# Routed experts in longer blocks: a first block of 256 rows, then blocks of up to 512 with the last in six lengths

## The chip, the cores and the metric

The kernel runs on one core of a Trainium2 chip. The metric is device time in microseconds (us) from one launch, the median of several runs. Before the change it is 1612.41 us, over three runs from 1605.84 to 1612.46.

## What is computed

Attention with a feature map, and then two mixtures of experts, one on the output of the other. There are 4608 tokens (8 batches of 576) of 512 values; each mixture has 8 experts with 512 x 1024 and 1024 x 512 weights, all in 32-bit floats, and a token goes to the one expert with the largest logit.

```python
def phi(x):                                   # attention
    proj = np.einsum('bhsd,df->bhsf', x, w_phi)
    proj = proj - np.max(np.abs(proj), axis=-1, keepdims=True)
    return np.concatenate([np.exp(proj), np.exp(-proj)], axis=-1)
q_p, k_p = (phi(q), phi(k))
kv = np.einsum('bhsf,bhsd->bhfd', k_p, v)
num = np.einsum('bhsf,bhfd->bhsd', q_p, kv)
den = np.einsum('bhsf,bhf->bhs', q_p, k_p.sum(axis=2))[..., None] + 1e-06
...
e_idx = np.argmax(x @ w_gate, axis=1)         # a mixture; it is applied twice
gate_w = probs[np.arange(N), e_idx]
eom = 1.0 / (1.0 + np.exp(-(x @ w_output_gate)))     # the first mixture alone
for e in range(E):
    mask = e_idx == e
    h = np.maximum(x[mask] @ w1[e], 0.0)
    out[mask] = gate_w[mask, None] * eom[mask, e, None] * (h @ w2[e])
```

## The kernel before, in words

**Stages.** Attention runs to about 495 us of the profiled span, the experts of the first mixture to about 1060, those of the second to the end. Attention also routes its own output: `logits` (L512) multiplies turned rows by the gate weights, `route` finds each token's expert, weight and rank, and `scatter` (L184) writes one table entry for each token into a table in HBM, in the place that the expert and the rank give. An expert's table entries say which rows of x to gather.

**A block.** `gather` (L287) fetches rows, 128 to a tile, by an indirect DMA from GpSimd; `turn` (L294) transposes them on TensorE (L301) and splits them into a high and a low part, on ScalarE (L303) and VectorE (L304). `block` (L307) takes 256 rows, or 128 with the high and low parts side by side. The hidden layer has eight chunks f of 128 units, and for each f and each of four chunks kc of x three matmuls (L328 to L330: high by high, low by high, high by low) or two (L333, L334). ScalarE and VectorE split the relu into hh and hl (L345, L346). The output layer makes 24 matmuls of 512 columns for each tile of 128 rows (L353 to L355); ScalarE multiplies the result by the token's weight (L359) and GpSimd scatters it (L360).

**A tail.** In the first mixture a finished block of two tiles is also routed for the second: `tail` (L369) turns its y (L381), multiplies by the gates (L391), adds up the four partial products with a matrix of ones (L399), lets `route` find places, and scatters two table entries. These steps are hooks in the next block: `hook(i)` runs them between its chunks f (0 to 7) and in its output layer (8 and up).

**The order.** Inside a block the program is put down as written. The first block of each expert carries, at hooks, the split of the next expert's weights (`split_steps`, L240: 8 chunks through four raw buffers, 512 KB each, refilled by SyncE), the turning of its own second block and of the next expert's first, and the gathers for the blocks after these, on GpSimd's queue. There are two sets of weights, `rings`, used in turn (w0.. and w1..). The table of all experts is read back once in a mixture, in `end_route` (L205) in the first block of expert 0.

**The chain of tests.** The number of rows of an expert is known only on the chip. After the first block each engine loads the counts into registers (L455), and `rest` (L466) tests them: more than 512 rows (L476) runs a full block and goes on; otherwise `short` (L482) chooses a block of 128, one of 256, or none. There is code for four such lengths (`FITTED`) and then a row of blocks of 256, each behind one test. Every engine that has work inside runs every test itself, and the code lies in the order of nesting.

Of the kernel before, what the change touches and what calls it, by code (L numbers as in the profile page):

```python
# [21 lines left out]
F32 = mybir.dt.float32  # L22
# [14 lines left out]
SLOTS = N // P  # L37
NG = B // 2
GW = P // KC
NT = 9  # L40
FITTED = 4


class Fused:
# [8 lines left out]
    def consts(self):  # L53
# [24 lines left out]
        self.pend = const.tile([P, 2], I32, name="pend")  # L78


    def new_route(self, name, n_scatter, pool, *gates):
# [13 lines left out]
        return {"name": name, "table": table, "rows": rows, "acc": acc,  # L95
# [94 lines left out]
    def early(self, r, psum):  # L190


        nc, sm = self.nc, self.small
        acc = r["acc"][:, 0:1]
        nc.tensor.matmul(psum[:, :1], self.ones_h, acc, start=True, stop=True)
        few = sm.tile([P, 1], F32, tag="few", name="few", bufs=1)
        nc.vector.tensor_scalar(few, psum[:, :1], float(2 * P), None, op0=ALU.is_lt)
        up = sm.tile([P, 1], F32, tag="up", name="up", bufs=1)
        nc.vector.tensor_scalar(up, acc, -1.0, 2.0, op0=ALU.mult, op1=ALU.add)
        nc.vector.scalar_tensor_tensor(acc, up, few, acc, op0=ALU.mult, op1=ALU.add)  # L200
        first = self.const.tile([P, 2, 2], I32, name=f"{r['name']}_first")
        nc.sync.dma_start(first, r["table"].rearrange("(p s) w -> p s w", p=P)[:, :2, :])
        r["first"] = first

    def end_route(self, r, psum):  # L205
# [3 lines left out]
        cnt = self.const.tile([P, E], I32, name=f"{r['name']}_cnt")  # L209
        bf = sm.tile([P, E], F32, tag="bf", name="bf", bufs=1)  # L210
        nc.vector.tensor_copy(bf, self.base_i)
        nc.vector.scalar_tensor_tensor(cnt, bf, -float(P), psum[:, :E], op0=ALU.mult, op1=ALU.add)
        nc.sync.dma_start(self.tab, r["table"].rearrange("(p s) w -> p s w", p=P))
        r["cnt"] = cnt


    def weight_buffers(self, pool, name):
        return [tuple(pool.tile([P, 1024], F32R, name=f"{name}{c}{x}") for x in "hl") for c in range(8)]
# [21 lines left out]
    def split_steps(self, i):  # L240

        nc = self.nc

        def step(c):
            raw = self.raws[c % 4]
            hi, lo = self.rings[i % 2][c]
# [7 lines left out]
    def weights(self, i):  # L254
        r = self.rings[i % 2]
# [5 lines left out]
    def expert_buffers(self, pool):  # L261

        self.ybuf = [pool.tile([P, D], F32, name=f"y{t}") for t in range(2)]
        self.xt = pool.tile([P, KC, 2 * P], F32, name="xt")
        self.ls = pool.tile([P, 2 * P], F32, name="ls")
        self.xg += [[self.shared.tile([P, D], F32, tag=tag, name=f"xg{i}{t}", bufs=2) for t in range(2)]
                    for i, tag in enumerate(("tl4", "phi1"), 1)]
        self.xbuf.append(pool.tile([P, KC, 2, 2 * P], F32R, name="x1"))
        self.hbuf = [self.shared.tile([P, FC, 2 * P], F32R, tag="phi4", name=f"h{x}", bufs=3) for x in "hl"]
        self.rings.append(self.weight_buffers(pool, "w1"))  # L270
# [560 lines left out]
```

## Time and profile before

| | before |
|---|---|
| median of 3 runs | 1612.41 us (1605.84 to 1612.46) |
| the profiled execution | 1597.7 us, span 1596.0 us |
| mean granted TensorE clock | 0.968 |
| PE (TensorE matmul) busy | 1488.2 us, 93% |
| PEld (weight load) busy | 1316.2 us, 82% |
| DVE (VectorE) busy | 737.0 us, 46% |
| ACT (ScalarE) busy | 589.5 us, 37% |
| POOL (GpSimd) busy | 424.6 us, 27% |
| DMA | 163.15 MB, mean 102 GB/s |

The page of the profile describes one execution; the span runs from its first instruction to its last. PE is TensorE's array, PEld its weight loads (beside the matmuls), PEldq and ACTq and so on the sequencers that feed an engine. A row of the trace names a line of the kernel, an engine, an operation and the tiles as out<-in. "Busy" of a matmul is from its start to a modelled end, so that consecutive ones overlap; the distance of two starts is the better price. "issue" as a releaser is time in which the engine waited for nothing that the profile shows. The granted clock is a share of TensorE's full speed.

### The profile page before, as it was taken

Reading aid. Unit: us, or ns where it says so; the run is one execution under the profiler, and the core shown is the slowest. Engines: PE = TensorE matmul, PEld = TensorE weight load, DVE = VectorE, ACT = ScalarE, POOL = GpSimd, SP = SyncE. Lnnn points to the kernel's source line nnn. Section 1 sums busy time; section 2 is a strip of 40 time slices with the busy share of each in tenths; the row PEclk is TensorE's granted clock in tenths of the full one; section 3 lists DMA queues with packets and bytes.
Section 4 is the critical chain, followed back from the end, with each engine's and each line's share of the span. In section 5 each row is a group of like instructions: output and inputs, shape, how many; then the busy total and the mean of one; then the engine's idle time right before and its main releaser. Section 6 shows DMA issues by size and latency. Waiting matters only on the chain.

```text
span 1596.0 us, 27799 instructions
## 1 busy us (share of the span) xinstructions
PE 1488.2 (93%) x10702; PEld 1316.2 (82%) x10702; DVE 737.0 (46%) x1939; ACT 589.5 (37%) x1199; POOL 424.6 (27%) x433
## 2 busy tenths in 40 slices
PE   7999899899999898998998999998989989998997
PEld 6887787787787797987987889887889879888986
DVE  6787576576665342625444536143144234141310
ACT  5554354354443232414333424132234334142311
POOL 3443533433443212312122212213112012110100
PEclk9999999999998999999999999999999989998999
DMA  7775123123013322404134404114144134131200
GB/s 204 240 244 188 46 61 127 47 67 126 24 38 128 117 70 99 162 24 151 62 115 135 147 26 146 43 41 165 41 155 160 42 125 163 42 116 68 86 19 28
DMA packets 99084, 163.15 MB, mean 102 GB/s; under 512 B 25819, under 2 KB 62043, under 8 KB 97760
## 3 DMA queue, kind: packets, MB, share of 16 engines
q1 hardware_dynamic: 83008, 117.98, 22.8%
q0 software_dynamic: 15776, 41.52, 7.7%
q8 instruction: 146, 2.39, 0.6%
q14 instruction: 154, 1.26, 0.3%
HBM read 118.67 MB, written 42.88 MB: 101 GB/s over the span
## 4 chain that ended last, share of the span: by engine, by line
PE 72%; issue 12%; DMA 9%; POOL 2%; ACT 2%; DVE 2%; SPq 0%; POOLq 0%; another core or an unknown queue 0%; ACTq 0%; DVEq 0%
DMA out_dram<-y,tab 7%; PE hp L328 7%; PE hp L330 7%; PE yp L353 7%; PE yp L355 7%; PE hp L329 7%; PE yp L354 7%; PE nm L672 6%; PE kvt L624 4%; PE pj L589 2%; PE hp L333 2%; PE tp L658 2%; PE pj L591 2%; PE pj L590 2%; PE tp L301 2%
## 5 line engine op out<-in xcount | busy, mean ns | idle before, releaser
L346 DVE SCALAR_TENSOR_TENSOR hl<-hp,hh 128x512 fp32r<-128x512 f32 x148 | 102.3, 691 | 336.1 <-ACT hh L345 336.1
L345 ACT ACTIVATE hh<-hp 128x512 fp32r<-128x512 f32 x148 | 88.5, 598 | 271.4 <-PE hp L330 252.2
L359 ACT ACTIVATE y<-yp,tab 128x512 f32<-128x512 f32 x76 | 52.4, 689 | 290.1 <-PE yp L355 225.2
L184 POOL DMA_INDIRECT r_table<-pay,at x78 | 78.6, 1008 | 291.8 <-DVE at L180 221.2
L360 POOL DMA_INDIRECT out_dram<-y,tab x38 | 38.4, 1010 | 411.0 <-ACT y L359 409.5
L672 PE MATMUL nm<-kvs,qt 128*128 128x65 f32 x1024 | 120.5, 273 | 3.3 <-DVE pre L140 1.5
L672 PEld LDWEIGHTS nm<-kvs,qt 128*128 128x128 f32 x1024 | 118.4, 192 | 4.9 <-issue 2.0
L593 DVE TENSOR_REDUCE am<-pj 128x4 f32<-128x512 f32 (+1 forms) x160 | 100.1, 634 | 33.7 <-PE pj L591 32.7
L594 DVE TENSOR_TENSOR d<-pj,am 128x512 f32<-128x512 f32 (+1 forms) x160 | 96.4, 629 | 2.5 <-PE kvt L624 2.4
L289 POOL DMA_INDIRECT xg<-r_rows,tab x82 | 86.2, 1052 | 40.2 <-issue 22.0
L589 PE MATMUL pj<-wh,th 128*128 128x256 f32 x288 | 88.3, 311 | 2.9 <-ACT th L576 1.5
L383 DVE COPY xt<-tp 128x512 f32<-128x512 f32 x21 | 14.5, 692 | 161.4 <-PE tp L381 161.4
L610 POOL TENSOR_TENSOR fs<-phi 128x512 f32<-128x512 f32 x32 | 40.8, 1275 | 180.7 <-ACT phi L603 147.4
L360 POOL DMA_INDIRECT r_rows<-y,tab x38 | 37.8, 994 | 188.7 <-ACT y L359 179.5
L660 ACT ACTIVATE qt<-tp 128x512 f32<-128x512 f32 (+1 forms) x192 | 79.5, 504 | 16.9 <-PE nm L678 8.3
L612 POOL TENSOR_TENSOR fs<-fs,phi 128x512 f32<-128x512 f32 x64 | 81.9, 1280 | 4.7
L590 PE MATMUL pj<-wl,th 128*128 128x256 f32 x288 | 83.0, 292 | 0.0
L591 PE MATMUL pj<-wh,tl 128*128 128x256 f32 x288 | 82.5, 299 | 0.3
L576 ACT CAST th<-tp 128x512 fp32r<-128x512 f32 (+1 forms) x96 | 42.1, 491 | 77.9 <-PE tp L572 77.8
L304 DVE TENSOR_TENSOR x<-tp,x 128x512 fp32r<-128x512 f32 x86 | 55.4, 683 | 26.6 <-ACT x L303 26.6
L328 PE MATMUL hp<-x,w10h 128*128 128x256 f32 x128 | 41.4, 324 | 27.2 <-issue 26.5
L589 PEld LDWEIGHTS pj<-wh,th 128*128 128x128 f32 x288 | 56.5, 196 | 11.0 <-ACT th L576 5.5
(293 smaller groups left out, 4620.5 us busy)
## 6 DMA issues: line engine op xcount, KB each, us to landing
raw<-in_moe_w_dram SPq DMA_DIRECT2D x128, 512.0 KB, 4.4
r_rows<-zero SPq DMA_DIRECT2D x15, 768.0 KB, 7.4
km<-in_k_dram SPq DMA_DIRECT2D x32, 256.0 KB, 3.0
qm<-in_q_dram SPq DMA_DIRECT2D x32, 256.0 KB, 3.6
vm<-in_v_dram SPq DMA_DIRECT2D x32, 256.0 KB, 3.4
r_rows<-x SPq DMA_DIRECT2D x8, 1024.0 KB, 4.8
xg<-r_rows,tab POOLq DMA_INDIRECT x82, 5.8
r_table<-pay,at POOLq DMA_INDIRECT x78, 2.2
```

The lines of the kernel that those rows point to most:

```text
L328: nc.tensor.matmul(o, w1h[kc][:, fs], x[:, kc, 0, :], start=first, stop=False)
L329: nc.tensor.matmul(o, w1h[kc][:, fs], x[:, kc, 1, :], start=False, stop=False)
L330: nc.tensor.matmul(o, w1l[kc][:, fs], x[:, kc, 0, :], start=False, stop=last)
L346: nc.vector.scalar_tensor_tensor(ol, hp, 0.0, oh.bitcast(F32), op0=ALU.max, op1=ALU.subtract)
L353: nc.tensor.matmul(yp, hh[:, f, sl], w2h[f], start=first, stop=False)
L354: nc.tensor.matmul(yp, hh[:, f, sl], w2l[f], start=False, stop=False)
L355: nc.tensor.matmul(yp, hl[:, f, sl], w2h[f], start=False, stop=last)
L589: nc.tensor.matmul(o, hi[:, i + j, :], wh, start=True, stop=False)
L590: nc.tensor.matmul(o, hi[:, i + j, :], wl, start=False, stop=False)
L591: nc.tensor.matmul(o, lo[:, i + j, :], wh, start=False, stop=True)
L593: nc.vector.tensor_reduce(am, pj, axis=AX.X, op=ALU.max, apply_absolute_value=True)
L672: nc.tensor.matmul(nm[:, t, :], qt[:, s, 4 * b + t, :], kv[:, 2 * b + s, :], start=(s == 0), stop=(s == 1))
```

## The change

- **Lengths.** Each expert's first block keeps 256 rows (`FIRST` tiles), with x in x0. What follows is in blocks of 512 rows, x in one buffer of four tiles, and the last one has 128, 256, 320, 384, 448 or 512 rows; a matmul of the hidden layer spans all of them. `end_route` computes for each expert how many half tiles and tiles are begun beyond the first block; the engines load both numbers.
- **The chain.** `choose` nests the tests: none left, at most 2 half tiles, 4, 5, 6, 7, 8, else a full block and a second choice of four lengths, and behind that a loop over blocks of 512.
- **Rows.** An expert's first block issues, ahead of its own matmuls, the gathers of the next four tiles and turns all four at hooks 10 to 19 (17 to 23 for expert 0). The expert's last block gathers and turns the next expert's first two tiles, at its hooks.
- **Weights.** There are three half sets, which change roles by `chunks`. The first block splits the next expert's w1 at hooks 1 to 7, the last block its w2; if there is none, both happen in `leave`, by themselves.
- **Tails** take the number of tiles of the block before them; ahead of a first block always four, with entries of no token in place of missing tiles. Buffers of y are four, aligned at their end, and set to zero at the start, like the unused parts of h, on GpSimd (`start_buffers`).
- **Logits.** The four partial products are turned by transposes and added by a reduce on VectorE, where a matmul by a matrix of ones did both; in attention (L525) and in the tails (L399).
- In PSUM, hp has three banks of one f each, tp three, yp two; before, hp had two tags of two banks, tp two, yp two.

```diff
     def end_route(self, r, psum):
...
+        nc.vector.tensor_scalar(cf, cf, -float(FIRST * P), 0.0, op0=ALU.add, op1=ALU.max)
+        for i, rows in enumerate((64, P)):
+            n = r["begun"][:, i, :]
+            nc.vector.tensor_scalar(n, cf, float(rows - 1), None, op0=ALU.add)
+            nc.vector.tensor_scalar(n, n, 6 + i, None, op0=ALU.logical_shift_right)
         nc.sync.dma_start(self.tab, r["table"].rearrange("(p s) w -> p s w", p=P))
-        r["cnt"] = cnt
+    def chunks(self, i):
+        sets = self.sets
+        return sets[(0, 2, 1)[i % 3]] + sets[(1, 0, 2)[i % 3]]
...
-        for fp in range(FC // 2):
-            hp = ps.tile([P, 2, 2 * P], F32, tag=f"hp{min(c, 1)}", name="hp", bufs=2)
...
+        for f in range(FC):
+            hp = ps.tile([P, 4 * P], F32, tag="hp", name="hp", bufs=3)
+            fs = slice(f * P, (f + 1) * P)
+            for kc in range(KC):
+                first, last = kc == 0, kc == KC - 1
+                if nt > 1:
+                    o = hp[:, :R]
+                    nc.tensor.matmul(o, w1h[kc][:, fs], x[:, kc, 0, :R], start=first, stop=False)
+                    nc.tensor.matmul(o, w1h[kc][:, fs], x[:, kc, 1, :R], start=False, stop=False)
+                    nc.tensor.matmul(o, w1l[kc][:, fs], x[:, kc, 0, :R], start=False, stop=last)
...
+        turns = {1: (9, 11, 13, 15), 2: (9, 11, 13, 15), 3: (10, 14, 18, 22), 4: (12, 17, 22, 27)}
+        splits = {1: (8, 10, 12, 14), 2: (8, 10, 12, 14), 3: (8, 12, 16, 20), 4: (9, 14, 19, 24)}
...
+        def part(g, t, size, before, final, rows=4):
...
+                if not final:
+                    self.gather(r, self.place(e, t + nt, rows))
+                    at(hooks, turns[nt], turn_steps(rows))
+                elif follow(g):
+                    at(hooks, (0, 0), follow(g))
+                    at(hooks, turns[nt], first_steps)
+                if not m:
+                    at(hooks, (0, 0, 1, 2, 4) if nt > 1 else (0, 0, 2, 4, 6), self.tail(r2, before, ps))
+                if final:
+                    at(hooks, splits[nt], self.split_steps(g + 1)[4:])
+                self.block(self.weights(g), self.x, self.place(e, t, nt), size * 64, dst, ps, hooks, not m)
...
+            def choose(sizes):
+                if not sizes:
+                    part(g, t, 8, before, False)
+                    rest(g, t + 4, done + 8, k, tiles, 4)
+                    return
+                with tc.If(k > done + sizes[0]) as more:
+                    choose(sizes[1:])
+                with more.Else():
+                    if sizes[0]:
+                        last(sizes[0])
+                    else:
+                        leave(g)
+            choose([0, 2, 4, 5, 6, 7, 8] if done == 0 else [2, 4, 6, 8])
...
+                if e:
+                    rows()
+                    at(hooks, (0, 0, 1, 2, 4), tail)
+                    at(hooks, (10, 13, 16, 19), turn_steps(4))
+                else:
+                    at(hooks, (0, 0, 1, 2, 3), tail)
...
+                    at(hooks, (4, 4), (lambda: self.end_route(r, col("cn")), rows))
+                    at(hooks, (17, 19, 21, 23), turn_steps(4))
+                at(hooks, (1, 3, 5, 7), self.split_steps(g + 1)[:4])
...
         for i in range(nt):
-            nc.tensor.matmul(lg[:, i, :], ls[:, i * P:(i + 1) * P], self.chunk_sum[:, :width],
-                             start=True, stop=True)
+            nc.tensor.transpose(lp[:, i * P:(i + 1) * P], ls[:, i * P:(i + 1) * P], self.ident)
+        nc.vector.tensor_reduce(
+            lg, lp.rearrange("p (t c e) -> p t e c", t=nt, c=KC)[:, :, :width, :], axis=AX.X, op=ALU.add)
```

How the rows of an engine move shows at two places, both where expert 1 of the first mixture goes from its first block to the next. First TensorE before the change: the last output matmuls (yp) of the first block, the register load, the first test, and the hidden layer (hp) of the second block with weights w1.. of that expert.

```order
5159 L353 MATMUL yp<-w17h,hh 128x512
5160 L354 MATMUL yp<-w17l,hh 128x512
5161 L355 MATMUL yp<-w17h,hl 128x512
5162 L455 TENSOR_LOAD r_cnt
5163 L476 COMPARE_AND_BRANCH
5164 L328 MATMUL hp<-x_6477,w10h 128x256
5165 L329 MATMUL hp<-x_6477,w10h 128x256
5166 L330 MATMUL hp<-x_6477,w10l 128x256
```

One load and one test stand ahead of the version with a full block of 256 columns. The same place after the change:

```order
4054 L376 MATMUL yp<-w03h,h_6488 128x512
4055 L377 MATMUL yp<-w03l,h_6488 128x512
4056 L378 MATMUL yp<-w03h,h_6490 128x512
4057 L546 TENSOR_LOAD r_begun x2
4058 L515 COMPARE_AND_BRANCH x7
4059 L353 MATMUL hp<-x,w20h 128x512
4060 L354 MATMUL hp<-x,w20h 128x512
4061 L355 MATMUL hp<-x,w20l 128x512
```

Two loads and seven tests now lie between them, and behind the tests stands the version for a full block of 512 that is not the last; each shorter version lies further on, where its test jumps to. Next GpSimd, before the change, in the output layer of that first block: table entries (r_table) of a tail, the scatters (r_rows) of the block's two tiles y, and gathers (xg) of rows.

```order
358 L184 DMA r_table<-pay,at 36864x2 x2
359 L360 DMA r_rows<-y_6469,tab 4609x512
360 L289 DMA xg_6473<-r_rows,tab 128x512
361 L289 DMA xg_6474<-r_rows,tab 128x512
362 L289 DMA xg_6119<-r_rows,tab 128x512
363 L289 DMA xg_6120<-r_rows,tab 128x512
364 L360 DMA r_rows<-y_6470,tab 4609x512
365 L455 TENSOR_LOAD r_cnt
366 L476 COMPARE_AND_BRANCH
```

Four gathers, for the next expert's second block and the first block of the one after it, stand between the two scatters, near the test. After the change:

```order
379 L320 DMA xg_6122<-r_rows,tab 128x512
380 L320 DMA xg_6123<-r_rows,tab 128x512
381 L320 DMA xg_6480<-r_rows,tab 128x512
382 L320 DMA xg_6481<-r_rows,tab 128x512
383 L189 DMA r_table<-pay,at 40960x2 x4
384 L383 DMA r_rows<-y_6484,tab 4609x512
385 L383 DMA r_rows<-y_6485,tab 4609x512
386 L546 TENSOR_LOAD r_begun x2
387 L515 COMPARE_AND_BRANCH x7
```

The four gathers, now for this expert's own next rows, come first, ahead of the tail's four table entries; between the scatters and the tests none is left.

## Rows read from the trace of the kernel before

**Rows 1.** The page, part 4: shares of the chain that ended last.
```profile
PE 72%; issue 12%; DMA 9%; POOL 2%; ACT 2%; DVE 2%; SPq 0%; POOLq 0%; another core or an unknown queue 0%; ACTq 0%; DVEq 0%
```

**Rows 2.** Groups of instructions: line, engine, tiles, xcount, busy us, mean ns, idle before.
```profile
L328 PE MATMUL hp<-x,w00h 128*128 128x256 f32 x168 | 51.9, 309 | 12.0 <-issue 11.4 <-DMA raw<-in_moe_w_dram 0.3 <-DVE lgs L714 0.3
...
L328 PE MATMUL hp<-x,w10h 128*128 128x256 f32 x128 | 41.4, 324 | 27.2 <-issue 26.5 <-PE yp L355 0.6
...
L333 PE MATMUL hp<-x,w00h 128*128 128x256 f32 x32 | 12.1, 378 | 1.5 <-ACT y L359 1.2 <-DVE xg L343 0.2
...
L301 PE MATMUL tp<-ident,xg 128*128 128x128 f32 x344 | 45.9, 275 | 6.8 <-DMA xg<-r_rows,tab 5.7 <-DVE x L304 1.1
...
L525 PE MATMUL lg<-chunk_sum,ls 128*128 128x16 f32 x72 | 10.7, 275 | 3.2 <-ACT ls L523 3.2
...
L383 DVE COPY xt<-tp 128x512 f32<-128x512 f32 x21 | 14.5, 692 | 161.4 <-PE tp L381 161.4
```

**Rows 3.** Stretches: us, busy of PE, PEld, DVE, ACT, POOL, PEclk, DMA share, GB/s.
```profile
637.45:651.03 13.58, 13.58 (x119) 12.99 (x117) 8.74 (x32) 6.75 (x13) 1.93 (x2) 1.00 0.23 75
...
1119.78:1131.27 11.49, 11.49 (x97) 11.49 (x96) 2.08 (x3) 2.48 (x4) 3.10 (x3) 1.00 0.20 70
...
1143.19:1151.00 7.81, 7.58 (x65) 7.43 (x65) 2.27 (x6) 2.95 (x7) 1.01 (x1) 1.00 0.12 42
```

**Rows 4.** Timeline of PE: start us, us, engine, line, operation, tiles.
```profile
1119.78 0.28 PE L328 MATMUL hp<-x,w00h 128*128 128x256 f32 x1
...
1131.17 0.28 PE L330 MATMUL hp<-x,w03l 128*128 128x256 f32 x1
...
1132.08 0.47 PE L353 MATMUL yp<-w04h,hh 128*128 128x512 f32 x1
...
1132.39 0.39 PE L354 MATMUL yp<-w04l,hh 128*128 128x512 f32 x1
...
1142.84 0.39 PE L355 MATMUL yp<-w07h,hl 128*128 128x512 f32 x1
```

**Rows 5.** Stretches again: the expert layers as a whole.
```profile
495.00:1589.60 1094.60, 1025.75 (x6659) 928.38 (x6659) 402.87 (x1057) 351.14 (x664) 216.50 (x211) 0.96 0.29 96
```

**Rows 6.** Waits of PE: waiting, releaser, us in total, times, longest.
```profile
PE hp L333 <- issue: 11.5, 3, 5.3
```

**Rows 7.** Sequencer of PE by line: xcount: shortest/median/longest ns, first to last start; waits.
```profile
L476 PEldq COMPARE_BRANCH  x27: 65/3423/6851, 522.6 to 1558.9; - x27
...
L483 PEldq COMPARE_BRANCH  x1: 6532/6532/6532, 604.7 to 604.7; - x1
...
L476 PEldq COMPARE_BRANCH  x1: 3730/3730/3730, 933.3 to 933.3; - x1
```

**Rows 8.** Timeline of PE at two joints between blocks; wait in brackets.
```profile
611.43 0.55 PE L328 MATMUL hp<-x,w10h 128*128 128x256 f32 x1 [7.12 <-issue]
...
937.12 0.39 PE L355 MATMUL yp<-w07h,hl 128*128 128x512 f32 x1
...
937.56 0.35 PE L333 MATMUL hp<-x,w00h 128*128 128x256 f32 x1
```

**Rows 9.** Stretches at those joints.
```profile
604.30:611.40 7.10, 0.00 (x1) 0.01 (x1) 0.48 (x4) 0.69 (x1) 2.05 (x2) 0.73 0.80 279
...
611.40:615.50 4.10, 4.07 (x23) 4.10 (x24) 0.15 (x1) 0.51 (x1) 0.00 (x0) 0.63 0.03 10
...
934.00:938.00 4.00, 3.95 (x20) 3.05 (x19) 0.00 (x0) 0.41 (x1) 0.10 (x1) 1.00 0.22 74
```

**Rows 10.** Timeline of ACT behind a jump; wait in brackets.
```profile
810.49 0.59 ACT L383 COPY xt<-tp 128x512 f32<-128x512 f32 x1 [5.77 <-issue]
...
1146.36 0.37 ACT L342 COPY xg<-hp 128x256 f32<-128x256 f32 x1 [2.36 <-issue]
```

**Rows 11.** The page, part 6: transfers: xcount, KB each, us from issue to landing.
```profile
raw<-in_moe_w_dram SPq DMA_DIRECT2D x128, 512.0 KB, 4.4
...
xg<-r_rows,tab POOLq DMA_INDIRECT x82, 5.8
```

More of the change, by code (lines that the diff above doesn't have):

```diff
@@ L94, in new_route @@
         nc.vector.tensor_copy(acc, self.base_i)
-        return {"name": name, "table": table, "rows": rows, "acc": acc,
+        own = {x: self.const.tile([P, *shape], I32, name=f"{name}_{x}")
+               for x, shape in (("first", (nt, 2)), ("begun", (2, E)))}
+        return {"name": name, "table": table, "rows": rows, "acc": acc, **own,
                 "gates": self.load_gates(f"{name}_gates", *gates), "views": iter(dram_disjoint_views(table, n_scatter))}
@@ L272, in first_rows @@
     def first_rows(self, r):
[L273 to L274 removed]
+        self.xg = [self.shared.tile([P, D], F32, tag="th4", name=f"xg{t}", bufs=2) for t in range(2)]
+        self.gather(r, r["first"])
     def first_turn(self, ps):
[L277 to L285 removed]
@@ L307, in block @@
-    def block(self, r, weights, x, e, c, nt, dst, ps, hooks, keep):
+        tp = ps.tile([P, KC, P], F32, tag="tp", name="tp", bufs=3)
+        for kc in range(KC):
+            nc.tensor.transpose(tp[:, kc, :], self.xg[t][:, kc * P:(kc + 1) * P], self.ident)
+        o = x[:, :, 0, t * P:(t + 1) * P]
+        nc.scalar.copy(o, tp)
+        nc.vector.tensor_tensor(x[:, :, 1, t * P:(t + 1) * P], tp, o.bitcast(F32), op=ALU.subtract)
+    def block(self, weights, x, place, R, dst, ps, hooks, keep):
@@ L421, in at, with turn_steps, follow @@
                 hooks.setdefault(i, []).append(f)
+        def turn_steps(n):
+            return [lambda t=t: self.turn(t, self.x, ps) for t in range(n)]
+        first_steps = [lambda t=t: self.turn(t, self.x0, ps) for t in range(FIRST)]
+        def follow(g):
+            m, e = divmod(g, E)
+            if g + 1 == 2 * E:
+                return None
+            if e + 1 < E:
+                return (lambda: None), (lambda: self.gather(mixes[m][0], self.place(e + 1, 0, FIRST)))
+            return (lambda: self.early(r2, col("early"))), (lambda: self.gather(r2, r2["first"]))
@@ L488, in experts @@
-            rest(1)
+            tail = self.tail(r2, 4, ps) if 0 < g <= E else []
+            rows = lambda: self.gather(r, self.place(e, FIRST, 4))
+            with tc.manual_schedule():
+                if e:
+                    rows()
+                    at(hooks, (0, 0, 1, 2, 4), tail)
+                    at(hooks, (10, 13, 16, 19), turn_steps(4))
+                else:
+                    at(hooks, (0, 0, 1, 2, 3), tail)
+                    if not m:
+                        at(hooks, [0], [lambda: [scatter() for scatter in left(col("rk"))]])
+                    at(hooks, (4, 4), (lambda: self.end_route(r, col("cn")), rows))
+                    at(hooks, (17, 19, 21, 23), turn_steps(4))
+                at(hooks, (1, 3, 5, 7), self.split_steps(g + 1)[:4])
+                self.block(self.weights(g), self.x0, self.place(e, 0, FIRST) if e else r["first"],
+                           FIRST * P, dst, ps, hooks, not m)
```

310 lines of the change are left out of this document (136 added, 174 removed).

## The prediction

> **What bounds the kernel now.** I read the chain of waits first. TensorE holds 72% of it and "issue", time in which nothing recorded is waited for, 12% [rows 1]. The second view counts TensorE's groups in the two MoE layers [rows 2]. Line 328 multiplies x by the chunk w00h or w10h once for each f, so 168 + 128 records, eight to a block, are 37 blocks of 256 rows; x32 at L333 is four blocks of 128 rows on the first weight set (two more ran on the other). That fits the rows that the router gives each expert, counted from the reference's inputs: 754, 436, 681, 421, 364, 417, 537, 998 in the first MoE and 852, 273, 572, 335, 915, 484, 677, 500 in the second. L301's 344 transposes are 86 gathered tiles turned, two of them before 495; L383's x21 counts the routing tails.
>
> The third view prices an undisturbed block [rows 3]: 11.49 us for the hidden layer of 256 rows, 13.58 with a routing tail in it (so a two-tile tail costs 2.09), 7.81 for 128 rows. The timeline prices one instruction [rows 4]. From 1119.78 to 1131.17 there are 95 steps of 0.120 us for 256 columns; from 1132.08 to 1142.84, 47 steps, the first 0.31 and the rest 0.227, for 512 columns. [...] Between 1131.17 and 1132.39 lie the last hidden matmul (0.12), eight transposes and one output matmul (0.23): 0.87 for the eight, 0.11 each, 0.45 a tile.
>
> The fifth view bounds the expert stretch, 495.0 to 1589.6 [rows 5]. Its dense work by these prices: 37 x 11.49 + 6 x 7.81 + 80 output tiles x 24 x 0.227 + 84 turned tiles x 0.45 + 21 tails x 2.09 = 989.5. The stretch lasted 1094.6, so **105 us are lost**. The idle times say where: 11.4 + 26.5 us wait for "issue" at L328 and 11.5 at L333, ahead of a block's first matmul, and 5.7 for gathered rows [rows 2, 6]. The rest is smaller waits and half clock after them.
>
> "issue" here is a branch. TensorE's sequencer records 65 ns for a test that falls through and 3.4 us in the median for one that jumps [rows 7]. A jump of 3.73 us at 933.3 cost almost nothing: the sequencer had reached it 3.8 us ahead of the last queued matmul (937.12), and the next block began at 937.56 [rows 7, 8]. [...] ScalarE has its own copy of every jump and no such lead: idle 2.4 us when quiet, 5.8 under load [rows 10].
>
> **The change, part by part.** *Hidden layer.* Now 16 first blocks of 256 rows; then by expert 512, 256, 448, 256, 128, 256, 320, 512+256 and 512+128, 128, 320, 128, 512+256, 256, 448, 256. On the line of [rows 4] a matmul of 512, 448, 320 columns takes 0.227, 0.200, 0.147, times 96. Sum: 23 x 11.49 + 4 x 21.8 + 2 x 19.2 + 2 x 14.1 + 4 x 7.81 = 449.2 against 472.0: **-22.8**. Of that, 704 fewer matmuls at 0.013 are 9.4 us; the rest is padding no longer multiplied. [...] The 0.120 and 0.227 [rows 4] are measured in this kernel, with its weight loads between them, so I go by them. The output layer keeps its 80 tiles.
>
> *Turned rows.* Every first block turns four tiles whether the expert has them or not: 106 tiles in the stretch for 84, **+9.9** on TensorE (the copies lie beside matmuls).
>
> *Tails.* Nine of four tiles (eight ahead of first blocks) and eight of two, for 21 of two. Logits by transposes save two of four small products in a two-tile tail: 1.87. For four tiles the matrix work alone is 3.3 (16 transposes, 4 products twice as long, 4 transposes, the ranks), twice a two-tile tail 4.18; the routing chain on VectorE and the weight splits share the same six microseconds, so I take 4.18: 52.6 for 43.9, **+8.7** (0 at the low end).
>
> *Attention.* Twelve times, 3 transposes replace 6 narrow products (72 at L525) [rows 2]: 36 x 0.11, **-4.0**; VectorE's reduce for a copy is off the path.
>
> *Losses.* Each expert is entered by two register loads and a chain of n tests, the last of which jumps over the longer versions. Loads and raw weights now start early: gathers at the head of the first block, the last weight chunk at its hook 7, 11 us ahead of the branch, where such transfers land in 4.4 and 5.8 us [rows 11]. So I take the quiet jump. TensorE then waits 2 x 0.42 (the record of 0.31 and a gap) + 3.4 + 0.2 - 3.83 = 0.6 us, and 0.13 for each of 53 further tests (twice the bare record): 16 x 0.6 + 6.9 = 16.7. In each MoE's first expert the last turn waits for a gather at the block's end, so nothing is queued ahead: 2 x 3.8 = 7.6. ScalarE arrives about 4 us behind the last matmul, and a tail's fourth tp bank needs its copy: 2.1 us in the 256-row blocks of the first MoE, 0.4 at 512, 12 in all, and 4 for 128-row blocks of the second. Exits: TensorE's jump hides behind its queue as at 937; far ones leave ScalarE late for four tails, 4 x 1.3 = 5. Three second choices: 4. Gathers: the 5.7 of before and 2 x 1.0 for two more scatters that GpSimd issues ahead of the table (1.93 for two) [rows 3]: 8. Half clock: twelve waits of the kind of 611 at 4.1 x (1 - 0.63) = 1.5 us: 18. Sum 75.3 for 105: **-29.7**. Bounds: 50, if jumps cost what 937 did; 112, if nothing is gained and loads and tests come on top. 75 lies nearest the quiet rows because what loads the DMA engines moves away.
>
> New memsets on GpSimd fall into its pauses while it waits for the last scatters; they cost nothing unless they push the table's load, 2 us at most. A third weight set moves the w2 splits into the last block, beside matmuls; eight copies of 0.59 and two evictions alike [rows 10] fill 5.9 us of ScalarE's time in the 10.9 of a 256-row block's output, and a 128-row one still holds 5.3 in 5.4.
>
> Sum: -22.8 + 9.9 + 8.7 - 4.0 - 29.7 = **-37.9**. The profiled execution took 1597.7, so 1560 by its own measure; the median of the runs, 1612.41, lies 14.7 above it, and I subtract from that: **1574.5 us**.
>
> **Rivals.**
> *Jumps vanish.* All are covered by queued matmuls as at 937: losses 50, 25 less: 1549. For it: the jump at 937 [rows 8]. [...]
> *Nothing gained at the joints.* ScalarE and VectorE, not TensorE's jump, start each block; losses stay at 105 to 112: 1604 to 1611, say 1608. For it: ScalarE's 5.8 us [rows 10].
> *Slower: the jumps stay loaded.* If weights and gathers are still moving when the 16 chains jump (DMA near the 80% of 604.30, not 22%), each takes about 6.1 us in place of 3.4 (43 us), ScalarE is 3.4 later in eight tails (27), and four more entries fall to half clock (6): +76, 1650. For it: 6.53 at 604.7. Against: the transfers' landing times.
> *The fixed cost doesn't shrink.* If the 0.013 us belongs to the columns or the weight load and grows with them, wide matmuls save only a fifth of 9.4 us, 7.5 less: 1582. Against: the two steps, 0.120 and 0.227, where such a cost would give 0.240 [rows 4]. [...]
>
> **How the numbers follow.** Forecast 0.60, vanishing jumps 0.12, nothing gained 0.15, loaded jumps 0.08, fixed cost 0.05. About 0.5%, 8 us, can be told from no change here. Range 1541 to 1610: from vanishing jumps with tails at no extra cost (1549 - 8.7) to the upper end of nothing gained; it leaves out the loaded jumps. Faster by over 0.5% (below 1604.3): the forecast but for 0.01, the vanishing jumps, the fixed cost, and 0.02 of nothing gained: 0.78. Same: 0.13. Slower: 0.09.
>
> **What would show it.** Right: 512-column hidden matmuls 0.227 apart; TensorE's branch records near 3.4 us at the entries with DMA below 30%; "issue" ahead of a block's first matmul about 25 us in all in place of 49; 106 tiles turned. Wrong: entries of 5 us and more; waits of TensorE for ScalarE's xt copies or ranks beyond 20 us; a block of 256 rows with a four-tile tail above 16 us.

## The result and the profile after

The changed kernel takes 1570.67 us in the median of four runs (1567.53 to 1571.97), the kernel before 1609.12 beside it: a ratio of 0.976, 95% interval 0.973 to 0.979. Measured again with 5 runs of its own (the run after_again below) it is 0.981, 0.978 to 0.983. So the change saves some 30 to 39 us; the forecast was 37.9, and 1574.5. The two profiled executions, 1597.7 and 1570.8 us, lie only 27 apart, because the profiled execution of before was 11 us faster than its own median. Terms of the forecast are compared with this pair of traces.

From the page of the changed kernel: the span, the busy shares and the chain that ended last.

```profile
span 1569.0 us, 27135 instructions
...
PE 1468.5 (94%) x10018; PEld 1256.0 (80%) x10018; DVE 766.5 (49%) x2038; ACT 623.7 (40%) x1342; POOL 465.5 (30%) x477
...
PE 60%; DMA 13%; issue 13%; DVE 5%; ACT 4%; POOL 3%; SPq 0%; another core or an unknown queue 0%; POOLq 0%; ACTq 0%; DVEq 0%
```

TensorE issues 684 matmuls less, and the others work a little more. The waits of TensorE answer to [rows 2, 6]:

```profile
PE hp L353 <- ACT y L382: 22.9, 21, 2.2
...
PE hp L353 <- issue: 8.1, 4, 2.2
PE tp L404 <- ACT xt L405: 5.2, 8, 1.8
PE hp L359 <- issue: 4.4, 1, 4.4
...
PE tp L330 <- DMA xg<-r_rows,tab: 4.3, 2, 2.3
```

"issue" ahead of a block's first matmul fell from 49.4 us to 12.5. In its place stand 21 waits put down to ScalarE's eviction of y (L382), which that matmul does not read. They are of two kinds. At thirteen exits (from an expert's last block to the next expert's first) the eviction does end last, 0.05 us ahead of the matmul: a wait that the forecast did not have. At the other eight, all entries (from a first block through the tests behind it), the record of the far jump ends later than the eviction, some 0.2 us ahead of the matmul, so there TensorE waits for the jump, whatever the releaser says. The stretches of single blocks (columns as in [rows 3]), hidden layers of 512, 320, 448 and 512 rows, and the expert layers as a whole, answer to [rows 3, 5]:

```profile
1086.12:1108.40 22.28, 22.06 (x96) 18.04 (x97) 5.51 (x8) 4.18 (x7) 4.85 (x5) 1.00 0.20 60
1217.94:1232.00 14.06, 14.06 (x96) 14.06 (x97) 3.35 (x7) 2.95 (x7) 3.01 (x3) 1.00 0.20 60
1468.11:1487.50 19.39, 19.39 (x96) 17.98 (x97) 4.37 (x7) 3.81 (x7) 2.67 (x3) 1.00 0.15 44
1320.52:1342.20 21.68, 21.68 (x97) 17.98 (x96) 4.84 (x7) 4.87 (x8) 5.11 (x5) 1.00 0.23 61
...
486.00:1559.60 1073.60, 1012.42 (x6011) 875.80 (x6011) 433.02 (x1154) 385.93 (x807) 257.98 (x248) 0.99 0.33 103
```

The wide blocks cost what was forecast (21.8, 14.1, 19.2), and TensorE ran the expert layers at a granted clock of 0.99, where it was 0.96.

The table shows where the 27 us come from, added up over all blocks from the starts of their matmuls (43 blocks before, 35 after). In the second mixture of the kernel before, the first 29 hidden matmuls of the next expert's first block already stand ahead of the test (1181.12 to 1184.47 is one such group, and 4.59 us of "issue" follow it); the wait behind them is counted here as one between blocks, and a normal step between blocks, 0.23 us, is not counted.

| | forecast | traces |
|---|---|---|
| hidden layers, by the prices of single blocks | -22.8 | -22.9 |
| tiles turned | +9.9 | +13.8 |
| attention, to the first hidden matmul (495.03, now 485.97) | -4.0 | -9.1 |
| tails, waits and half clock, in three places: | -21.0 | -11.9 |
| - inside hidden layers (tails among them) | | -1.2 |
| - from a block's last yp matmul to the next block's first hp | | -18.4 |
| - inside output layers (the first block of each mixture: rows not yet there, lower clock) | | +7.7 |
| behind the last matmul (span's end) | 0 | +3.0 |
| rest (rounding) | | +0.1 |
| sum | -37.9 | -27.0 |

### The profile page after: what moved, and what is told of

Read it like the earlier page. It is cut to its first block, busy times and chain, and to the rows that moved or that the text cites. A ratio compares the mean times of both kernels' runs of the same rounds, so it can differ in the third digit from the quotient of the medians.

```text
span 1569.0 us, 27135 instructions
## 1 busy us (share of the span) xinstructions
PE 1468.5 (94%) x10018; PEld 1256.0 (80%) x10018; DVE 766.5 (49%) x2038; ACT 623.7 (40%) x1342; POOL 465.5 (30%) x477
## 3 DMA queue, kind: packets, MB, share of 16 engines
q14 instruction: 191, 1.56, 0.3%
## 4 chain that ended last, share of the span: by engine, by line
PE 60%; DMA 13%; issue 13%; DVE 5%; ACT 4%; POOL 3%; SPq 0%; another core or an unknown queue 0%; POOLq 0%; ACTq 0%; DVEq 0%
DMA xg<-r_rows,tab 6%; PE nm L734 6%; PE yp L376 6%; PE yp L378 6%; PE yp L377 6%; PE hp L353 5%; PE hp L354 5%; PE hp L355 5%; PE kvt L686 4%; DMA out_dram<-y,tab 3%; PE pj L651 2%; PE tp L330 2%; PE pj L653 2%; PE pj L652 2%; PE tp L720 2%
## 5 line engine op out<-in xcount | busy, mean ns | idle before, releaser
L368 DVE SCALAR_TENSOR_TENSOR h<-hp,h 128x256 fp32r<-128x256 f32 (+3 forms) x248 | 116.3, 474 | 376.4 <-ACT h L367 360.0
L367 ACT ACTIVATE h<-hp 128x256 fp32r<-128x256 f32 (+3 forms) x248 | 105.2, 425 | 311.4 <-PE hp L355 249.8
L333 DVE TENSOR_TENSOR x<-tp,x 128x512 fp32r<-128x512 f32 x108 | 74.6, 691 | 168.3 <-ACT x L332 160.4
L189 POOL DMA_INDIRECT r_table<-pay,at x88 | 93.7, 1065 | 209.0 <-DVE at L185 135.2
L320 POOL DMA_INDIRECT xg<-r_rows,tab x104 | 109.6, 1054 | 141.6 <-PE hp L355 49.6
L332 ACT CAST x<-tp 128x512 fp32r<-128x512 f32 x108 | 63.3, 587 | 139.3 <-PE tp L330 120.7
L382 ACT ACTIVATE y<-yp,tab 128x512 f32<-128x512 f32 x76 | 52.3, 688 | 157.8 <-PE yp L378 133.5
L383 POOL DMA_INDIRECT r_rows<-y,tab x38 | 37.9, 997 | 190.4 <-ACT y L382 190.4
L330 PE MATMUL tp<-ident,xg 128*128 128x128 f32 x432 | 65.7, 275 | 4.3 <-DMA xg<-r_rows,tab 4.3
L330 PEld LDWEIGHTS tp<-ident,xg 128*128 128x128 f32 x432 | 54.1, 142 | 19.3 <-issue 3.3
```

The lines of the kernel that those rows point to most:

```text
L320: self.nc.gpsimd.indirect_dma_start(self.xg[t][:, :], None, r["rows"], bass.IndirectOffsetOnAxis(ap=place[:, t, 0:1], axis=0), bounds_chec ...
L330: nc.tensor.transpose(tp[:, kc, :], self.xg[t][:, kc * P:(kc + 1) * P], self.ident)
L367: nc.scalar.activation(oh, o, AF.Relu)
L368: nc.vector.scalar_tensor_tensor(ol, o, 0.0, oh.bitcast(F32), op0=ALU.max, op1=ALU.subtract)
```

## Experiments

Ratios are against the kernel before, on the same chip, with 95% intervals; the changed kernel itself is 0.976 in the first measurement and 0.981 in the second.

**Loads moved back to the tests.** In the main loop, where the first block splits w1:

```diff
-at(hooks, (1, 3, 5, 7), self.split_steps(g + 1)[:4])
+at(hooks, (14, 17, 20, 22), self.split_steps(g + 1)[:4])
```

> The first block splits the next expert's w1 at hooks 14 to 22 in place of 1 to 7, so the refills, four of 512 KB, are on the DMA engines while the tests of the 16 experts are run. Theory: code is fetched by the same engines, so the far jumps at the entries take 5 to 6.5 us in place of 3.3 to 3.9, TensorE waits about 2 us more at each, and some blocks begin at half clock: +30 to +45, 1600 to 1616; the gain of the change over the kernel before is mostly gone. Rival: the jumps of before were slow for another reason (their distance or number), and the entries stay as they are: 1571 within 5.

Measured: 0.9925 (0.9897 to 0.9953), so about two thirds of the gain are gone: 19 to 27 us, short of the 30 to 45 expected. Two entries of the changed kernel, from the start of the far jump to the first matmul behind it, in the view of stretches:

```profile
593.87:597.89 4.02, 2.49 (x11) 1.72 (x10) 0.77 (x3) 1.02 (x2) 0.48 (x1) 1.00 0.02 6
...
1171.76:1175.30 3.54, 2.61 (x12) 1.82 (x11) 0.69 (x1) 1.14 (x2) 0.00 (x0) 1.00 0.02 7
```

The tests there in the records of TensorE's sequencer (columns as in [rows 7]), the far jump the longest:

```profile
L515 PEldq COMPARE_BRANCH  x3: 65/77/3854, 593.6 to 593.9; - x3
...
L515 PEldq COMPARE_BRANCH  x1: 3378/3378/3378, 1171.8 to 1171.8; - x1
```

With the late loads, two entries in the view of stretches:

```profile
733.84:738.96 5.12, 2.08 (x11) 1.38 (x9) 3.13 (x7) 2.69 (x5) 0.98 (x1) 0.93 0.81 256
...
1185.95:1191.31 5.36, 2.26 (x10) 1.53 (x9) 3.10 (x5) 2.87 (x6) 1.01 (x1) 1.00 0.82 259
```

And their jumps in the records of the sequencer:

```profile
L515 PEldq COMPARE_BRANCH  x1: 4950/4950/4950, 733.8 to 733.8; - x1
...
L515 PEldq COMPARE_BRANCH  x1: 5197/5197/5197, 1185.9 to 1185.9; - x1
```

The DMA engines are 2% busy at the entries of the changed kernel and over 80% here, and the same jump takes 5.2 us in place of 3.4 (the second entry of each). Of the thirteen entries with a far jump twelve take 4.2 to 5.2 us; the last expert's, which has no weights to refill, finds the DMA engines 2% busy and takes 3.6. The packets in the trace show where the time goes: each of these four jumps holds one packet of 16 KB on a queue of instructions. At the second entry it begins 1.04 us behind the jump's start in the changed kernel and 2.84 us behind it here, and takes 0.96 us in both. All distances between blocks grow by 20.8 us, and the hidden layers by 10.8, part of it at a lower clock. That is the rival "the jumps stay loaded", brought about by one edit, and it confirms the step that carried the losses: the jumps are cheap because the loads were moved away from them. That a jump waits for this packet is argued from its place inside each of them and from the two delays, 1.04 us at 2% of DMA and 2.84 at 82%; no run shows it by itself.

**Halves.** Each matmul of over 256 columns becomes two:

```diff
+cut = [0, R] if R <= 2 * P else [0, R // 2, R]
+for a, b in zip(cut, cut[1:]):
+    for kc in range(KC):
...
-o = hp[:, :R]
+        o = hp[:, a:b]
```

> Each hidden layer of over 256 rows is computed in two halves of its columns, one after the other, so 8 blocks have 96 matmuls more each, and nothing else changes. If a matmul pays 13 ns beside its columns, as forecast: 768 x 0.013 = +10, 1581. [...] If the price of 256 columns is proportional, 0: 1571.

Measured: 1.0007 (0.9969 to 1.0045), 30 to 40 us above the changed kernel, not 10. Stretches of a hidden layer of 512, 320 and 448 rows, in halves:

```profile
1356.92:1379.90 22.98, 22.98 (x193) 22.97 (x192) 4.84 (x7) 4.87 (x8) 5.12 (x5) 1.00 0.22 58
...
1231.55:1270.30 38.75, 37.49 (x192) 37.45 (x193) 3.44 (x7) 3.06 (x7) 3.06 (x3) 0.57 0.07 23
1509.18:1530.70 21.52, 21.52 (x193) 21.52 (x194) 4.37 (x7) 3.82 (x7) 2.76 (x3) 1.00 0.13 40
```

For 512 rows it is 22.98 against 21.68: +1.30 for 96 matmuls, 13.5 ns each, as forecast. Matmuls of 224 columns, however, are 0.112 us apart (21.52 / 192), and in the first mixture those of 160 columns also take 0.112 in the median (23.7 us for 192 and a tail): at both widths the step is the same, where the forecast's line would go on down, to 0.107 and 0.080. At 224 columns PEld, the weight load, is busy throughout (21.52 of 21.52 us). And the 320-row block at 1231 ran at a granted clock of 0.57 for its whole 38.75 us. Of the 40 us by which the eight layers grow in this trace, 32 are in the two of 320 rows. So the expectation failed by two costs that it left out; its 13 ns held.

**What the exits wait for.** The last eviction of an expert is shared out:

```diff
+half = D // 2 if final and t == nt - 1 else D
+nc.scalar.activation(y[:, :half], yp[:, :half], AF.Copy, scale=place.bitcast(F32)[:, t, 1:2])
+if half < D:
+    nc.vector.tensor_scalar(y[:, half:], yp[:, half:], place.bitcast(F32)[:, t, 1:2], None, op0=ALU.mult)
```

> In the last block of an expert, the last eviction of y (0.69 us on ScalarE) is split into two halves of 256 columns, one on ScalarE and one on VectorE. Theory: at the exits TensorE waits for the last thing that ScalarE and VectorE did in the version, though it reads none of it, so 1.22 us from the last yp to the next hp matmul becomes 0.9 at 15 exits: -5, ratio 0.973. Rival: TensorE waits for the branch or for x0: 1.22 stays.

Measured: 0.985 (0.983 to 0.988), slower than the changed kernel beside it by 10 us. An exit of the changed kernel in the timeline, of TensorE and then of ScalarE:

```profile
1440.79 0.39 PE L378 MATMUL yp<-w03h,h 128*128 128x512 f32 x1
1442.00 0.39 PE L353 MATMUL hp<-x,w10h 128*128 128x256 f32 x1 [0.83 <-ACT y L382]
1442.22 0.28 PE L354 MATMUL hp<-x,w10h 128*128 128x256 f32 x1
...
1441.26 0.69 ACT L382 ACTIVATE y<-yp,tab 128x512 f32<-128x512 f32 x1 [4.75 <-PE yp L378]
```

The same exit with the split, in the timeline of TensorE, ScalarE and VectorE:

```profile
1445.36 0.39 PE L378 MATMUL yp<-w03h,h 128*128 128x512 f32 x1
1446.36 0.38 PE L353 MATMUL hp<-x,w10h 128*128 128x256 f32 x1 [0.61 <-ACT y L383]
1446.88 0.39 PE L354 MATMUL hp<-x,w10h 128*128 128x256 f32 x1
...
1445.84 0.47 ACT L383 ACTIVATE y<-yp,tab 128x256 f32<-128x256 f32 x1 [4.75 <-PE yp L378]
...
1446.34 0.48 DVE L385 TENSOR_SCALAR y<-yp,tab 128x256 f32<-128x256 f32 x1 [5.03 <-ACT y L383]
```

The eviction on ScalarE is 0.22 us shorter, and the first matmul comes 0.21 earlier (1.00 for 1.21). But the halves ran one behind the other, and the second matmul, which reads the low part of x that VectorE wrote, now waits for VectorE's half: 1.52 against 1.43. So the theory holds (the first matmul of the next expert waits for whatever ScalarE did last in the version, the second for VectorE) and the edit fails: most exits are 0.2 us shorter, but the hidden layers behind them are up to 0.4 longer at full clock (12.02 for 11.61). Over all blocks the distances fall by 3.3 us against after_again and the hidden layers grow by 14.1, some at a lower clock (two of 14.5 us at 0.88, for 13.0 and 12.4 at full clock); whether the split brings that about isn't shown. The order of the two waits also points to x0 and not to the bank of hp: the first matmul reads what ScalarE wrote of x0 and the second what VectorE wrote, while hp is used by both engines and the first matmul starts 0.46 us before VectorE's half ends.

**Taking that wait away** was tried three times. own_hp gave first blocks a PSUM bank of their own, in two halves; own_first also turned the next expert's first rows ahead of the tests; own_first2 used the bank for every third chunk only:

```diff
+if e < E - 1:
+    at(hooks, (9, 11), [lambda t=t: self.gather(r, self.place(e + 1, t, 1), t) for t in range(FIRST)])
+    at(hooks, (19, 21), first_steps)
...
+lone = own and f % 3 == 0
+hp = ps.tile([P, 4 * P], F32, tag="hp0" if lone else "hp", name="hp", bufs=1 if lone else 2)
```

> Only the bank of first blocks is apart (and the versions have two banks in place of three); x0 is still written inside the versions. Theory: one of the two reasons is enough, so the 1.22 us at the exits stay and the time is 1571 within 4; should the bank alone have been the reason, the exits fall to 0.3 and the time to 1557. If two banks are too few for the versions, their hidden layers grow: by up to 1 us in each of 16, 1585.

> Theory: TensorE stands 1.0 us at each of 15 exits, because the next expert's x0 and the PSUM banks of hp were last touched inside versions of different lengths, and so its first matmul waits for ScalarE to finish the whole version, whose last work is the eviction of y. Here six of the eight experts of each mixture turn the next expert's first rows in their own first block, ahead of the tests, and first blocks have a bank of their own, so neither is touched inside a version: the distance from the last yp matmul to the next hp matmul falls from 1.22 us to 0.3 at 12 exits, about -10 us, 1560. Rival: the wait has another reason (y itself, the branch): the distance stays at 1.22 and the time at 1571. Second rival: the two turns crowd the first block's output, which gives back 5 us: 1566.

> As own_first, but first blocks share no bank among their own chunks: every third chunk f has a bank hp0 that no version of the tests touches, the others use the two banks of the versions; the next expert's first rows are turned at hooks 19 and 21. Theory: the wait for ScalarE at the exits is one for the whole version, so with x0 and the bank of f = 0 settled ahead of the tests the first matmuls of the next first block need not wait at all: 12 exits of 1.22 us fall to 0.3, -11 us, 1560. What the two turns add to the first block they take out of the last. Rival: what is won at the exits is lost at the entries, because the gathers now land close to the tests and their far jumps take over 4 us: 1571 or above.

Measured: 1.050 (1.044 to 1.056), 1.100 (1.093 to 1.108) and 1.009 (1.005 to 1.013). In own_hp the exits stayed at 1.22, as the theory said; the time went elsewhere: two chunks in one bank are one tile to the program, so each chunk waits for the eviction of the one before it (99.8 us over 100 waits for VectorE; in own_first, which has the same bank, 101.8 over 95). A group of TensorE's instructions in own_hp, the hidden layers of first blocks on one weight set:

```profile
L353 PE MATMUL hp<-x,w00h 128*128 128x256 f32 x72 | 26.4, 367 | 49.2 <-DVE h L368 39.1 <-ACT y L382 6.4 <-issue 3.3
```

In own_first2 nothing of the next first block depends on the versions any more, and so the scheduler put its first 12 hidden matmuls ahead of the tests. They wait for x0, which is turned just ahead. TensorE's sequencer stood with them, began the far jump only 0.16 us ahead of the last of them, and all of it came out on the array. The far jumps of the entries take 3.3 to 4.2 us, little more than in the changed kernel, so the rival's load is not the reason. The record of the sequencer in own_first2:

```profile
L516 PEldq COMPARE_BRANCH  x1: 3673/3673/3673, 600.5 to 600.5; - x1
```

And TensorE's timeline there:

```profile
600.66 0.28 PE L356 MATMUL hp<-x,w13l 128*128 128x256 f32 x1
604.23 0.39 PE L354 MATMUL hp<-x,w20h 128*128 128x256 f32 x1 [3.30 <-issue]
```

At the exits themselves the wait is gone. In the second mixture five of the six exits that were prepared so are one normal step long, as here in TensorE's timeline:

```profile
1216.98 0.39 PE L379 MATMUL yp<-w13h,h 128*128 128x512 f32 x1
1217.21 0.28 PE L354 MATMUL hp<-x,w20h 128*128 128x256 f32 x1
```

The sixth has a jump of 6.0 us, and in the first mixture the tail's transposes come to stand there (2.6 us). So the wait for ScalarE can be taken away, which bears out its cause, and in this kernel it comes back, and more, at the entries: a jump is hidden only as far as the sequencer was ahead (0.16 us here, 3.8 at the exit of the changed kernel whose test starts at 1506.4 and whose last output matmul starts at 1510.18).

**One register load less.** The second count is loaded only in front of the loop that reads it.

```diff
-begun = [[nc.values_load(r["begun"][0:1, j, i:i + 1], min_val=0, max_val=N // (64 << j))
-          for j in range(2)] for i in range(E)]
+load = lambda j, i: nc.values_load(r["begun"][0:1, j, i:i + 1], min_val=0, max_val=N // (64 << j))
+begun = [load(0, i) for i in range(E)]
...
-with tc.For_i(done // 2, tiles, 4) as i:
+with tc.For_i(done // 2, load(1, e), 4) as i:
```

> The second register, which only the loop behind two full blocks reads, is loaded there and no longer ahead of each chain of tests. TensorE's sequencer runs a fixed distance ahead of the array, and at an entry it has used that up, so each thing it does ahead of the far jump comes out on the array: one load of 0.30 us and its gap less, and the distance from the last output matmul to the next hidden one, 1.3 to 2.0 at the entries, falls by 0.4 at 14 of 16: -6, ratio 0.972. Rival: ScalarE or VectorE, not TensorE's sequencer, starts each block, and nothing changes: 0.976.

> The changed kernel once more, without an edit. Two profiled executions, 1597.7 before and 1570.7 after, are 27 us apart, while the medians are 38.5 apart. If the execution of before that was profiled happened to have few stretches at half clock, the ratio stays at 0.976 with a narrower interval, and this profile's parts (joints, hidden layers, turns) agree with the first within 5 us in all. If instead the first measurement was favourable to the change, the ratio rises to 0.983.

Measured side by side: 0.9765 (0.9741 to 0.9789) and 0.9807 (0.9782 to 0.9833); 1559.83 us (1558.64 to 1562.02) and 1564.62 (1563.67 to 1570.82). One entry in TensorE's timeline, without the edit:

```profile
1168.53 0.39 PE L378 MATMUL yp<-w13h,h 128*128 128x512 f32 x1
1170.09 0.36 PE L359 MATMUL hp<-x,w00h 128*128 128x256 f32 x1 [1.18 <-ACT y L382]
```

The same entry in one_load:

```profile
1167.60 0.39 PE L378 MATMUL yp<-w13h,h 128*128 128x512 f32 x1
1168.58 0.36 PE L359 MATMUL hp<-x,w00h 128*128 128x256 f32 x1 [0.59 <-issue]
```

1.56 us became 0.98 (0.58 less); over eleven entries behind first blocks the mean is 0.39 less, as expected, and a twelfth, 4.21 us in after_again and 4.74 in the first trace, became 0.89. That one is not the register load. In both traces its jump ends over 3 us ahead of the matmul, and in that gap a second packet of 16 KB comes on the queue of instructions (at 1276.95 in the first trace, 0.92 us); the other twelve entries of the first trace have one such packet, inside the jump. late_loads, with as much code, has the second packet too; in one_load, split_evict, best, exact_tails, exact_turns and halves it is missing, and the entry is 0.9 to 1.6 us long. So it goes with where the code lies (argued, not tested), and some 3 us of what one_load and the two edits under "Padding" gain are not their own. Among the kernels that are not fitted to these inputs one_load has the lowest time, 1559.83 us; its ratio is that of the first measurement of the change. As for after_again, its parts agree with the first trace to 5 us, and the ratio lies between the two cases that it was to tell apart: the first measurement was a little favourable to the change, and the profiled execution of before a fast one.

**best** adds the split and a later second half of the tail's transposes:

```diff
-at(hooks, (0, 0, 1, 2, 4) if nt > 1 else (0, 0, 2, 4, 6), self.tail(r2, before, ps))
+at(hooks, (0, 1, 2, 3, 5) if nt > 1 else (0, 1, 2, 4, 6), self.tail(r2, before, ps))
```

> Both edits, and the tail in a version begins its second pair of transposes one chunk later (hooks 0, 1, 2, 3, 5), so that its fourth bank does not wait for ScalarE's first copy: 5.2 us over eight waits in the changed kernel. Sum: -6 - 5 - 4 = -15, about 1555, ratio 0.967. If ScalarE, late behind its own jump, is what the tail waits for, the shift brings half of its 4.

Measured: 0.980 (0.977 to 0.983), a miss. The distances between blocks fall by 9.8 us against after_again, but hidden layers grow by 8.0, with the split's second wait among them and more first blocks at a granted clock of 0.80 to 0.88. The shift by itself was not run.

**Padding.** exact_tails and exact_turns write into the code what these inputs need: two tiles in five of the tails ahead of first blocks, and only the turns of tiles that exist.

```diff
-tail = self.tail(r2, 4, ps) if 0 < g <= E else []
+tail = self.tail(r2, (4, 2, 4, 2, 2, 2, 4, 2)[g - 1], ps) if 0 < g <= E else []
```

```diff
+tiles = (4, 2, 4, 2, 1, 2, 3, 4, 4, 1, 3, 1, 4, 2, 4, 2)[g]
-at(hooks, (10, 13, 16, 19), turn_steps(4))
+at(hooks, (10, 13, 16, 19), turn_steps(tiles))
```

> The tail ahead of five of the first blocks (and of the second mixture's first) routes two tiles in place of four, as these inputs need; which ones is written into the code, so it fits these inputs alone. A four-tile tail costs 4.1 to 5.3 us in the trace and a two-tile one at least 2.1: by the forecast's price -2.1 for each of five, -10, 1560. Rival: the tail is bound by the chain from engine to engine and not by its matrix work, so two tiles take as long: 1570.

> First blocks of experts other than the first turn only the tiles that these inputs have behind the first 256 rows, 35 of 56; the gathers stay. Each tile is priced at 0.47 us of TensorE: 21 fewer, -10, 1561. Rival: TensorE gets ahead of what it waits for next (the jump, ScalarE's last eviction), and half of it comes back there: 1566.

Measured: 0.974 (0.971 to 0.978) and 0.971 (0.968 to 0.975). Both lie at or below the second measurement of the change; from the first exact_tails can't be told, so the stretches decide. In the changed kernel, a first block's hidden layer with a tail of four tiles, and an output layer with four tiles turned:

```profile
625.27:640.80 15.53, 15.23 (x126) 14.05 (x127) 9.90 (x37) 7.55 (x17) 5.36 (x6) 1.00 0.40 130
...
583.33:596.00 12.67, 12.67 (x66) 10.40 (x64) 5.83 (x12) 4.45 (x8) 5.20 (x5) 1.00 0.43 138
```

The same hidden layer in exact_tails, with a tail of two:

```profile
623.96:637.80 13.84, 13.71 (x116) 12.88 (x117) 8.93 (x35) 6.86 (x17) 6.04 (x6) 1.00 0.45 140
```

And the same output layer in exact_turns, with two tiles turned:

```profile
583.13:594.90 11.77, 11.77 (x58) 9.62 (x56) 4.36 (x10) 3.27 (x6) 5.83 (x5) 1.00 0.45 143
```

Two tiles less in a tail are worth 1.69 us, two tiles less turned 0.90. The rival for the tails falls; their price was 2.09 in the forecast's block of 256 rows, 2.31 by its own 4.18 and 1.87. The rival for the turns falls too: the entries behind did not grow (the ten behind fewer turns are 0.9 to 1.5 us in exact_turns, 1.3 to 2.0 in the changed kernel but for the long one).

**Attention alone.** The kernel before, with the logits of attention by transposes:

```diff
-nc.tensor.matmul(lg[:, i, :], ls[:, i * P:(i + 1) * P], self.chunk_sum[:, :width],
-                 start=True, stop=True)
+nc.tensor.transpose(lp[:, i * P:(i + 1) * P], ls[:, i * P:(i + 1) * P], self.ident)
...
+nc.vector.tensor_reduce(
+    lg, lp.rearrange("p (t c e) -> p t e c", t=nt, c=KC)[:, :, :width, :], axis=AX.X, op=ALU.add)
```

> The kernel before with one part of the change alone, the logits of attention by transposes and a reduce (twelve times; the tails stay as they were). The forecast's term was -4.0, 36 x 0.11 us. In the trace of the changed kernel the first hidden matmul comes 9.1 us earlier. If that is all due to the logits, the first hidden matmul comes at 486 and the time falls by 9; if the logits are worth 4 to 5 and the rest was a stretch at half clock in the one execution, 4 to 5: 1602 against 1606.

Measured: 0.9948 (0.9924 to 0.9973), -8.3 us, with -4 at one end of the interval. In its one trace the first hidden matmul comes only 0.8 us earlier than before:

```profile
494.19 0.58 PE L328 MATMUL hp<-x,w00h 128*128 128x256 f32 x1 [0.45 <-DVE lgs L527]
```

The traces differ in stretches of attention at a lower clock, here at 0.83:

```profile
416.00:436.00 20.00, 16.77 (x131) 14.32 (x132) 8.39 (x21) 6.45 (x17) 9.62 (x10) 0.83 0.12 32
```

The kernel before had one at 0.89:

```profile
170.00:200.00 30.00, 26.87 (x221) 23.07 (x220) 14.77 (x39) 9.83 (x23) 18.02 (x22) 0.89 0.22 60
```

The changed kernel ran these 30 us at full clock:

```profile
170.00:200.00 30.00, 26.87 (x249) 23.13 (x249) 17.28 (x45) 12.05 (x27) 18.82 (x22) 1.00 0.23 60
```

The twelve traces with the changed attention have their first hidden matmul anywhere from 484.6 to 491.1 us, so the 9.1 of one pair of traces is not the price of the transposes. The part is worth 4 to 12 us in the runs; how much is the transposes and how much is clock stays open.

## Why the prediction was right, and where its steps were not

- **Hidden layer, -22.8: right.** 512, 448 and 320 columns take 0.227, 0.203 and 0.147 us, forecast 0.227, 0.200 and 0.147 on the line through two steps, 0.120 for 256 columns and 0.227 for 512. The sum by the traces is -22.9. The 13 ns of each matmul are 2 x 0.120 - 0.227, an estimate from these steps, and the halves show them by themselves, as 13.5. The rival "the fixed cost doesn't shrink" is out.
- **Turned rows, +9.9: right in kind, +13.8 in size.** 106 tiles were turned, as forecast, but a tile costs 0.49 between output matmuls, where nearly all of them now lie, and 0.45 was read where two stand together.
- **Tails, +8.7: the price of two more tiles was 1.69, not 2.09**, but 2.4 to 4.2 for a two-tile tail (from the lengths of the second blocks of over 128 rows), not 1.87: ScalarE comes late to its xt copies (5.2 us over eight waits), as the forecast's losses had it. One of its signs of being wrong appeared: of the nine hidden layers of 256 rows with a tail of four tiles, four took over 16 us (16.9, 16.9, 18.1 and 20.2, the last two at a granted clock of 0.91 and 0.83).
- **"I take the quiet jump": right.** Quiet is a jump like the one at 933, with DMA at 22% [rows 9]. The far jumps of thirteen entries take 3.3 to 3.9 us, at 2% of DMA where it was read; with the loads moved back they take up to 5.2. The entries cost 25.1 us above a normal step (adding up the sixteen), and 24.3 were forecast. That the sums are so near is partly luck: 4.5 of the 25.1 are the one long entry with two packets of instructions, and the first entry of each mixture took 4.3 for the two, where 7.6 were forecast.
- **"Exits: TensorE's jump hides behind its queue": this step failed.** At thirteen of the fifteen the jump does hide, but the first matmul behind it waits for ScalarE's last eviction, 1.0 us at most of them and 14.2 in all. At the other two the jump itself took 6.2 and 5.9 us, with the DMA engines 73 and 74% busy, and came out on the array, 4.3 for the two. That is 18.5 us, where the forecast had nothing on TensorE and 5 on ScalarE. The kernel before has 1.2 us of this kind in all; its first blocks touched neither x0 nor their bank of hp inside a version, and the change moved both there. split_evict points to x0, and own_hp shows that the bank alone does not settle it.
- **Nothing was forecast behind the last matmul**: GpSimd's last scatter begins at 1560.79 and the span ends 8.2 us later; before it was 5.2. Why stays open.
- **Half clock, 18: not far off.** Its 4.1 us at 0.63 are the one stretch of before that starts at 611.40 [rows 9], and from 608 to 613 the granted clock was 0.50; that twelve waits bring such a stretch was an estimate, and no run shows it. The granted clock of the expert layers went from 0.96 to 0.99. By the trace's record of the clock it is 0.986, so over 1073.6 us at most 15 were lost to it (an estimate from the two).
- **Attention, -4.0: at the low end**, 4 to 12 in the runs.

The total came out nearer than its parts. By the pair of traces the sum was 11 us too large: tails, waits and half clock gave back 11.9 where 21.0 were forecast, the turns cost 4 more and the end 3 more, and attention gave 5 more on the other side. By the medians of the two measurements it was right in the first and 7 too large in the second. So it is partly luck that 1570.67 lies so near 1574.5: the time that the forecast started from, 1612.41, is above the medians that the kernel before had beside the runs, 1595 to 1609. The rival "nothing gained at the joints" is out, as 18.4 us were gained there, and "jumps vanish" by the entries. The "loaded jumps" came at two exits and at no entry, as late_loads shows for the reason that was given.

## What to carry over

In this kernel a data-dependent jump cost TensorE what its sequencer had not already run ahead of (up to 3.8 us): keep transfers, register loads and semaphore waits out of the last few us ahead of it, and look at the DMA share there first. Moving a buffer's last use into a branch made its next user wait for the last thing that the buffer's writer did in the branch (1.0 us at most exits), even with no data in common; look in the trace for a wait whose releaser writes nothing that the waiter reads. A sum of terms can land on the time by errors of both signs, so check the terms against the traces, and check which execution the trace is.

## Not expected

Transposes of 128 columns and matmuls of 160 and 224 columns are all 0.11 us apart in this kernel. Each brings its own 128-column weights, and PEld is busy 21.52 of 21.52 us at 224 columns; that the weight load sets the step is argued from this. And a whole hidden layer of such matmuls, with TensorE busy 37.49 of 38.75 us, ran at a granted clock of 0.57 in halves; why stays open. Ten runs of that kernel spread from 1595.76 to 1615.57.
